# A three-stage mixer (decayed attention, two MLPs): attention products in whole float32, and the decays' range tests moved behind it

## The chip, the cores and the metric

One core of a Trainium2 chip runs the whole program in one launch. The time is device microseconds of that core, the median of 3 runs.

## The reference

Batch 4, 8 heads, 768 steps, head size 48 (384 = 8 x 48 channels).

```python
mag = np.sqrt(a_re**2 + a_im**2); scale = np.minimum(mag, 0.999) / (mag + 1e-6)
a = (a_re + 1j * a_im) * scale                       # decay per step and channel
for t in range(768):                                 # attention: a state per head
    S = a[t][:, None] * S + k[t][:, None] * v[t]     # complex S
    y[t] = q[t] @ S.real
x = y                                                # first MLP, with a low-rank mix over time
u = x + (x^T U V)^T;  x1 = u + relu(u @ w1) @ w2     # 384 -> 1536 -> 384
u = x1 + real(fft2(x1)); n = layernorm(u)            # second MLP
out = u + relu(n @ v1) @ v2
```

All inputs are float32, and the U, V and the weights of both MLPs arrive as 64-bit floats that the kernel turns into 32-bit ones itself.

## The kernel before, in words

Time is cut into chunks of 128 steps, 6 for a batch. `decays(m)` and `turns(m)` make, for a pair of chunks, the cumulated decay (a running product, L398) and the cumulated angle (a running sum, L440) and multiply both into q and k: the tile `QK`, which six transfers (L481) lay out as `QT` with the heads along the free axis. `products(m, j)` then does a chunk's matrix products: scores `sc` from `QT`, masked scores `pm`, the output `y` from `pm` and v and from the carried state `S`, and the state's growth `g` from the transposed key `k` and v.

Precision is kept in two ways. Batches 0 and 1 (`plain`) compute `y` in float32, each head in two halves of 64 columns. Batches 2 and 3 split both factors into a float16 part and its float16 rest (`ph`, `qh`, `vh`, `vl`, `Sh`, `Sl`) and add three float16 products. The growth `g` is made of three float16 products in all batches, from `scaled`, a copy of the key times the chunk's end decay (ACT, L477). ACT makes the float16 parts, and DVE the rests.

The MLPs (`moe_units`) run batch after batch in 24 units (2 halves of the sequence x 12 blocks of 128 hidden channels). A unit is 9 float16 products into `hp`, a relu split into `hh` (ACT, L232) and `hl` (DVE, L233), and 9 products into `acc` (L214, L215, L200). The attention of batch b+1 is interleaved with the first MLP of batch b. With the first MLP of batch 3 run the Fourier transform of batch 0 (`dft`) and the conversion of the second MLP's weights (`weights(1)`): 24 pieces `stw` are loaded as 64-bit words (L129), and ACT, DVE (L122, L144, L145) and GpSimd (L167, L168) turn each into `w`.

Order on each engine is set by a scheduler, which takes the instructions in the order of the code and by priority, and lets one with less priority go ahead where its inputs are there and the buffers free. What runs first is then fixed. A pool's tag names a ring of buffers: tag `u` (5 buffers) holds the MLP's input pieces `u` (three alive at a time), the loaded weight pieces `stw` and the keys `k` of batch 0.

Range tests leave sums and maxima in `stats`, and `verdict` reads them at the end: whether the decays lie in the range that the method allows (inside `decays`, L345 to L371) and whether the weights do (`check_w`, L178).

Of the kernel before, what the change touches and what calls it, by code (L numbers as in the profile page):

```python
# [22 lines left out]
DM = H * D  # L23
# [5 lines left out]
KSCALE = 2.0**10  # L29
VSCALE = 2.0**10  # L30
GSCALE = 2.0**-10
YSCALE = 2.0**-10 / FSCALE
# [18 lines left out]
def mixer_kernel(ctx, tc, a_in, qk_in, v_in, u_in, v4_in, w_in, cc_in, ss_in, cb_in, sb_in, id_in, mask_in, rows_in, out):  # L51
# [26 lines left out]
    def pair(name):  # L78
        return moe.tile([128, 2, 384], F16 if parts16[0] else F32R, tag="u", name=name, bufs=5)
# [92 lines left out]

    def check_w(mi, f, z):

        hi = wt[mi, f][:, 0, z * 384 : (z + 1) * 384]
        unread = ft(f"chk{mi}_{f}_{z}", [128, 384], BF16, tag="chk", bufs=2)
        at = stats[:, list(BOUNDS).index(("w1", "w2")[z]), mi * FB + f : mi * FB + f + 1]
        V.scalar_tensor_tensor(out=unread, in0=hi, scalar=1.0, in1=hi, op0=ALU.mult, op1=ALU.mult, accum_out=at)  # L178
# [11 lines left out]
    def moe_units(mi, uT, finish, extra, batches=range(B)):  # L190
# [53 lines left out]
        "im": [(ALU.is_le, 0.0)],  # L244
# [68 lines left out]
    def decays(m):  # L313
# [17 lines left out]
        ew[m] = T_, Th, qf, kf, ends, a if b == 0 else turn, qk if b == 0 else ls  # L331
# [4 lines left out]
        def unread(js):  # L336
            n = (js.stop - js.start) * 384
            return slot(f"un{m}").bitcast(BF16)[:, :n].rearrange("p (i j t) -> p i j t", i=3, t=128)

        at_once = b or m in (0,1,)  # L340

        def steady(js):

            re, s2_ = of(js, a[:, 0], s2)
            V.scalar_tensor_tensor(  # L345
                out=unread(js), in0=s2_, scalar=RE_LEAST, in1=re, op0=ALU.add, op1=ALU.is_le, accum_out=stat("re", b, cc[js.start])
            )

        def least_re(js):

            (re,) = of(js, a[:, 0])
            V.tensor_scalar(unread(js), re, RE_LEAST, 0.0, ALU.is_ge, ALU.add, accum_out=stat("re", b, cc[js.start]))

        def most_im(js):
            (s2_,) = of(js, s2)
            V.tensor_scalar(unread(js), s2_, IM_MOST**2, 0.0, ALU.subtract, ALU.max, accum_out=stat("im", b, cc[js.start]))

        for js in jj:
            re, im, s1_, s2_ = of(js, a[:, 0], a[:, 1], s1, s2)
            if at_once:  # L360
                if b == 0:
                    V.scalar_tensor_tensor(out=s2_, in0=im, scalar=0.25, in1=im, op0=ALU.mult, op1=ALU.mult)
                else:
                    A.activation(s2_, im, AF.Square, scale=0.5)
                A.activation(s1_, re, AF.Square, accum_out=stat("big", b, cc[js.start]))
                if m == 0:
                    steady(js)
                else:
                    unused = unread(js) if b == 0 else Th[:, :, js]
# [3 lines left out]
            else:  # L373
                (V if m == 0 else G).tensor_tensor(s2_, im, im, ALU.mult)
                A.activation(s1_, re, AF.Square, accum_out=stat("big", b, cc[js.start]))
                (G if m == 2 else V).tensor_tensor(s1_, s1_, s2_, ALU.add)
                most_im(js)
# [3 lines left out]
        for js in jj:  # L381
# [4 lines left out]
            if not at_once:  # L386
                least_re(js)
# [35 lines left out]
    def turns(m):  # L423
# [3 lines left out]
        T_, Th, qf, kf, ends, turn, scaled = ew[m]  # L427
# [6 lines left out]
        for js in jj:  # L434
# [31 lines left out]
            for j in range(js.start, js.stop):  # L466
                c = cc[j]
                where = dict(pl=early[0], bufs=1) if b == 0 and c % 3 == 2 else dict(bufs=2)
# [13 lines left out]
                qkt[b, c] = QT, scaled[:, :, :, j]  # L482
                yield

    def products(m, j):
# [5 lines left out]
        plain = b <= 1  # L491
        at = attention_pool()

        def t3(nm, bufs, shape, dt=F32):
            return at(f"{nm}{n}", nm, bufs, shape, dt, attp[1] if dt == F16 else attp[0])

        QT, scaled = qkt[b, c]
        vin = inp["v", b, c]
        sc, pm, kp = [], [], []
        pool = pacc if b == 0 else pms  # L500

# [7 lines left out]
        def masked(hf):  # L509
            pm.append(room[:, hf] if b == 0 else at(f"pm{n}_{hf}", "pm", 2, (128, 4, 128)))  # L510
            V.tensor_tensor(pm[hf], sc[hf], mask.unsqueeze(1).to_broadcast([128, 4, 128]), ALU.mult)
            if not plain:
                hs = slice(hf * 4, hf * 4 + 4)
                A.copy(ph[:, hs], pm[hf])
                V.tensor_tensor(plo[:, hs], pm[hf], ph[:, hs], ALU.subtract)

        def turned(z):
            kp.append(bank(f"kp{n}_{z}", pool)[:, :384])
            for i in range(3):
                T.transpose(kp[z][:, i * 128 : (i + 1) * 128], scaled[:, z, i], ident)  # L520

        def split(z):
            src = kp[z].rearrange("t (x h) -> t h x", h=8)
            dh, dl = (k.rearrange("t (h z x) -> t h z x", h=8, z=2)[:, :, z, :] for k in (kh, kl))
            A.activation(dh, src, AF.Copy, scale=KSCALE)
# [768 lines left out]
```

## Time and profile before

| | |
|---|---|
| median of 3 runs (lowest, highest) | 995.34 us (994.02, 997.83) |
| the profiled execution: own time, span | 995.69 us, 993.9 us |
| busy in the span: PE, DVE, ACT, POOL | 819.1, 669.9, 465.4, 259.9 us |

The span is the time from the first to the last instruction of the profiled execution. PE is the matrix engine (PEld its weight loads), DVE the vector engine, ACT the scalar engine, POOL is GpSimd, SP issues transfers. Busy times of engines overlap each other.

### The profile page before, as it was taken

The numbers are of one execution on the slowest core, as the hardware profiler recorded it, in microseconds if no ns is written. First come the engines' busy times: TensorE is split into PE (matmuls) and PEld (weight loads), VectorE is DVE, ScalarE is ACT, GpSimd is POOL, SyncE is SP. The second block draws the span as 40 slices with busy tenths as digits, with TensorE's granted clock in tenths as the row PEclk, the third lists the DMA queues.
The fourth block names the chain that finished last, engine by engine and source line by source line (L and its number), as shares of the span: only waits on it lengthen the run. The fifth ranks groups of instructions, "written<-read, shape, count | busy, mean of one in ns | idle before, by whom it ended". The sixth has DMA issues, their size and how long they took to land.

```text
span 993.9 us, 16380 instructions
## 1 busy us (share of the span) xinstructions
PE 819.1 (82%) x6350; PEld 550.5 (55%) x6350; DVE 669.9 (67%) x1214; ACT 465.4 (47%) x897; POOL 259.9 (26%) x275
## 2 busy tenths in 40 slices
PE   0056667777897886989979799879999999999997
PEld 0045534556565654656656466446666765666564
DVE  7966797867567787858876996995645454463221
ACT  8546457576775867767753253332222211312111
POOL 4412474412012010111102644761322132020000
PEclk9999878888998999999989999999999999999999
DMA  9059646453743727264262632420101021000000
GB/s 360 1 64 146 159 130 139 106 101 97 115 90 81 111 73 128 68 102 86 37 89 74 221 96 87 145 64 24 50 31 48 1 80 50 1 25 1 25 24 28
DMA packets 47095, 83.41 MB, mean 84 GB/s; under 512 B 5600, under 2 KB 36064, under 8 KB 47008
## 3 DMA queue, kind: packets, MB, share of 16 engines
q1 hardware_dynamic: 45152, 75.96, 34.0%
q0 software_dynamic: 1856, 6.31, 1.8%
q8 instruction: 52, 0.85, 0.4%
q14 instruction: 35, 0.29, 0.1%
HBM read 53.79 MB, written 9.44 MB: 64 GB/s over the span
## 4 chain that ended last, share of the span: by engine, by line
PE 37%; DVE 30%; DMA 13%; ACT 9%; issue 5%; SPq 3%; POOL 2%; DVEq 0%; ACTq 0%; POOLq 0%
DMA QT<-QK 8%; PE acc L214 5%; PE acc L200 5%; PE acc L215 5%; PE hp L105 5%; PE hp L107 5%; PE hp L106 5%; DMA stw<-in_w_dram 4%; SPq L481 3%; DVE ls L398 2%; DVE wxw L145 2%; DVE wxw L144 2%; PE sc L506 2%; DVE hl L233 2%; DVE chk L178 2%
## 5 line engine op out<-in xcount | busy, mean ns | idle before, releaser
L214 PE MATMUL acc<-w,hh 128*128 128x384 f16 x576 | 194.5, 338 | 26.4 <-ACT hh L232 25.1
L233 DVE SCALAR_TENSOR_TENSOR hl<-hp,hh 128x384 f16<-128x384 f32 x192 | 105.1, 550 | 156.1 <-ACT hh L232 155.3
L232 ACT ACTIVATE hh<-hp 128x384 f16<-128x384 f32 x192 | 92.7, 484 | 231.9 <-PE hp L107 214.2
L215 PE MATMUL acc<-w,hh 128*128 128x384 f16 x576 | 193.6, 337 | 0.0
L200 PE MATMUL acc<-w,hl 128*128 128x384 f16 x576 | 128.8, 332 | 1.0 <-DVE hl L233 1.0
L105 PE MATMUL hp<-u,w 128*128 128x384 f16 x288 | 95.1, 333 | 13.3 <-ACT u L691 8.3
L506 PE MATMUL sc<-QT 96*128 96x128 f32 x384 | 62.8, 324 | 45.2 <-DMA QT<-QK 25.2
L106 PE MATMUL hp<-u,w 128*128 128x384 f16 x288 | 95.4, 331 | 2.2 <-DVE u L692 2.2
L214 PEld LDWEIGHTS <-hh 128*128 128x128 f16 x576 | 57.9, 100 | 69.8 <-ACT hh L232 33.8
L105 PE MATMUL hp<-n,w 128*128 128x384 f16 x288 | 93.9, 326 | 1.5 <-DVE hl L233 1.5
L107 PE MATMUL hp<-u,w 128*128 128x384 f16 x288 | 94.7, 330 | 0.0
L106 PE MATMUL hp<-n,w 128*128 128x384 f16 x288 | 93.9, 326 | 0.0
L107 PE MATMUL hp<-n,w 128*128 128x384 f16 x288 | 93.9, 326 | 0.0
L506 PEld LDWEIGHTS sc<-QT 96*128 96x128 f32 x384 | 57.6, 230 | 50.3 <-issue 40.8
L106 PEld LDWEIGHTS <-w 128*128 128x128 f16 x576 | 56.7, 98 | 43.9 <-issue 10.2
L105 PEld LDWEIGHTS <-w 128*128 128x128 f16 x576 | 56.8, 99 | 43.3 <-issue 7.7
L200 PEld LDWEIGHTS <-hl 128*128 128x128 f16 x576 | 57.1, 100 | 41.6 <-issue 3.7
L107 PEld LDWEIGHTS <-w 128*128 128x128 f16 x576 | 56.7, 98 | 39.6 <-issue 4.3
L215 PEld LDWEIGHTS <-hh 128*128 128x128 f16 x576 | 58.0, 101 | 35.9 <-issue 6.4
L581 POOL TENSOR_SCALAR fe<-QT 96x8 f32<-96x8 f32 x20 | 5.2, 263 | 215.2 <-DMA QT<-QK 215.2
L168 POOL TENSOR_TENSOR w<-wxw,w 128x384 f16<-128x384 f32 x48 | 54.1, 1131 | 3.1
L520 PE MATMUL kp<-ident,qkin 128*128 128x128 f32 x30 | 6.1, 338 | 55.0 <-ACT qkin L477 53.9
(290 smaller groups left out, 1728.0 us busy)
## 6 DMA issues: line engine op xcount, KB each, us to landing
QT<-QK SPq DMA_DIRECT2D x144, 129.0 KB
stw<-in_w_dram SPq DMA_DIRECT2D x48, 384.0 KB
ain<-in_a_dram SPq DMA_DIRECT2D x12, 768.0 KB
qkin<-in_qk_dram SPq DMA_DIRECT2D x12, 768.0 KB
x1d<-x SPq DMA_DIRECT2D x24, 192.0 KB
vin<-in_v_dram SPq DMA_DIRECT2D x18, 192.0 KB
lo<-x1d SPq DMA_DIRECT2D x12, 192.0 KB
out_dram<-lo SPq DMA_DIRECT2D x12, 192.0 KB
```

The costliest lines, as they stand in the source:

```text
L105: T.matmul(o, ah, bh, start=start, stop=False, skip_group_check=skip)
L106: T.matmul(o, ah, bl, start=False, stop=False, skip_group_check=skip)
L107: T.matmul(o, al, bh, start=False, stop=stop, skip_group_check=skip)
L144: V.scalar_tensor_tensor(out=xi, in0=xi, scalar=3, in1=low, op0=ALU.logical_shift_left, op1=ALU.bitwise_or)
L168: G.tensor_tensor(w[:, 1, zs], x, w[:, 0, zs], ALU.subtract)
L200: T.matmul(acc[t], hl[:, t * 128 : (t + 1) * 128], w2h, start=False, stop=f == FB - 1 and extra is None)
L214: T.matmul(acc[t], hh[:, ts], w2h, start=f == 0, stop=False)
L215: T.matmul(acc[t], hh[:, ts], w2l, start=False, stop=False)
L232: A.activation(hh, hp, AF.Relu)
L233: V.scalar_tensor_tensor(out=hl, in0=hp, scalar=0.0, in1=whole_of(hh), op0=ALU.max, op1=ALU.subtract)
L481: nc.sync.dma_start(QT[p0 : p0 + 16], QK[:, z, i, :])
L506: T.matmul(ps[:, h, :], q[:, 128:256], q[:, :128], start=True, stop=True)
```

## The change

All products of the attention become float32: `y` in all batches as before in batches 0 and 1, and `g` from the whole key and v, in two halves (64 and 32 columns). The float16 parts and rests of scores, queries, values, keys and state go. The key is transposed as it is in `QK`; the end decay is applied to the state after the growth is added (it was applied to the old state before). The tests of the decays leave `decays`; `check_a` loads the decays once more and tests them, in code that stands in the second MLP's first batch. Buffers: `stw`, the keys `k` of all batches and the decays of `check_a` share a ring `st` of 3; `u` has its 5 to itself; the third `QK` and `QT` buffer, that batch 0 had, is there for all batches.

```diff
     def fetch(src, name):
-        st = moe.tile([128, 384, 2], I32, tag="u", name=f"st{name}", bufs=5)[:, :n]
+        st = moe.tile([128, 384, 2], I32, tag="st", name=f"st{name}", bufs=3)[:, :n]
...
+    def check_a(m, z):
+
+        b, cc = PAIRS[m]
+        x = moe.tile([128, 768], F32, tag="st", name=f"rl{m}_{z}", bufs=3)
+        nc.sync.dma_start(x, a_in[b, cc[0] // 2][:, z].rearrange("p i j t -> p (i j t)"))
+        unread = slot(f"chka{m}_{z}").bitcast(BF16)
+        if z == 0:
+            V.tensor_scalar(unread, x, RE_LEAST, 0.0, ALU.is_ge, ALU.add, accum_out=stat("re", b, cc[0]))
+            A.activation(unread, x, AF.Square, accum_out=stat("big", b, cc[0]))
+        else:
+            for c, sign in zip(cc, (1.0, -1.0)):
+                V.tensor_scalar(unread, x, sign, 0.0, ALU.mult, ALU.max, accum_out=stat("im", b, c))
...
-                    A.activation(unused, re, AF.Relu, bias=least, scale=-1.0, accum_out=stat("im", b, cc[0]))
-                    A.activation(unused, s2_, AF.Relu, bias=most, accum_out=stat("im", b, cc[1]))
-                V.scalar_tensor_tensor(out=s1_, in0=s2_, scalar=4.0, in1=s1_, op0=ALU.mult, op1=ALU.add)
...
+            A.activation(s2_, im, AF.Square)
+            A.activation(s1_, re, AF.Square)
+            (G if m == 2 else V).tensor_tensor(s1_, s1_, s2_, ALU.add)
...
-                if c != NC - 1:
-                    for i in range(3):
-                        A.activation(scaled[:, :, i, j], QK[:, :, i, 128:256], AF.Copy, scale=ends[:, i, j : j + 1])
...
-            A.activation(dh, src, AF.Copy, scale=KSCALE)
-            V.scalar_tensor_tensor(out=dl, in0=src, scalar=KSCALE, in1=dh, op0=ALU.mult, op1=ALU.subtract)
+            A.copy(ks.rearrange("t (h z x) -> t h z x", h=8, z=2)[:, :, z, :], src)
...
-            ops = [(lambda h: ph[:, h], vh), (lambda h: ph[:, h], vl), (lambda h: plo[:, h], vh)]
-                ops += [(lambda h: qh[:, h], shi), (lambda h: qh[:, h], slo), (lambda h: ql[:, h], shi)]
-        summed(yp, ops, halves=plain)
+        summed(yp, ops)
...
-            summed(gp, [(hs(0), vh), (hs(0), vl), (hs(768), vh)])
+            summed(gp, [(lambda h: ks[:, h * 96 : (h + 1) * 96], vin)])
...
-                V.scalar_tensor_tensor(out=sS, in0=gp[:96], scalar=scale, in1=sS, op0=ALU.mult, op1=ALU.add)
+                V.scalar_tensor_tensor(out=sS, in0=gp, scalar=FSCALE, in1=S, op0=ALU.mult, op1=ALU.add)
+                V.tensor_tensor(by_head(sS), by_head(sS), f3, ALU.mult)
...
+        if b == 0 and half == 1:
+            check_a(f, g)
```

Three places in the order of the instructions. First DVE in the attention of batch 2, chunks 1 and 2, while the first MLP works on batch 1 (`hl`). Before:

```order
L526 SCALAR_TENSOR_TENSOR k_1_2979<-kp_1_1_3004,k_1_2979 128x8x48
L372 SCALAR_TENSOR_TENSOR ls_4_3159<-ls_4_3159 128x768
L556 SCALAR_TENSOR_TENSOR vl_2_3214<-vin_2_3012,vh_2_3213 128x384
L619 SCALAR_TENSOR_TENSOR S_1_3097<-g_1_3096,S_1_3097 96x384
L608 TENSOR_TENSOR S_2_3372<-S_1_3097,fe_2_3278 96x384
L233 SCALAR_TENSOR_TENSOR hl_1_0_5_2920<-hp_1_0_5_2902,hh_1_0_5_2919 128x384
L565 TENSOR_TENSOR ql_2_3232<-QT_2_2988,qh_2_3231 96x1024
L511 TENSOR_TENSOR pm_2_0_3227<-sc_2_0_3208,mask 128x512
L624 TENSOR_TENSOR Sl_1_3131<-S_1_3097,Sh_1_3130 96x384
```

After:

```order
L546 SCALAR_TENSOR_TENSOR S_1_2851<-g_1_2828,S_0_2684 96x384
L547 TENSOR_TENSOR S_1_2851<-S_1_2851,fe_1_2761 96x384
L446 TENSOR_TENSOR QK_4_3080<-ls_4_2879,turn_4_2878 128x6x128 x2
L244 SCALAR_TENSOR_TENSOR hl_1_0_2_2523<-hp_1_0_2_2512,hh_1_0_2_2522 128x384
L359 SCALAR_TENSOR_TENSOR ls_0_3259<-ls_0_3259 128x768
L480 TENSOR_TENSOR pm_2_0_2940<-sc_2_0_2926,mask 128x512
L244 SCALAR_TENSOR_TENSOR hl_1_0_3_2562<-hp_1_0_3_2535,hh_1_0_3_2561 128x384
```

The rests are gone from DVE's queue, and the masked score of chunk 2 stands three units earlier in the MLP.

Second the transfer queue (SP) where the second MLP's weights begin to be loaded. Before:

```order
L481 DMA QT_5_4969<-QK_5_4967 16x8x258 x6
L851 DMA rows<-in_rows_dram 128x5
L861 DMA lo_0_5704<-x1d_75 128x384
L861 DMA lo_1_5705<-x1d_75 128x384
...
L129 DMA stw_0_0_5663<-in_w_dram 128x768
L129 DMA stw_0_1_5720<-in_w_dram 128x768
```

After:

```order
L450 DMA QT_5_4383<-QK_5_4381 16x8x258 x5
L309 DMA vin_5_4603<-in_v_dram 128x384
L127 DMA stw_0_0_4967<-in_w_dram 128x768
L127 DMA stw_0_1_5024<-in_w_dram 128x768
L127 DMA stw_1_0_5079<-in_w_dram 128x768
```

The weights now follow the last `QT` directly, ahead of the Fourier transform's loads.

Third DVE early in the first MLP's last batch (units 3 to 7 of batch 3). Before:

```order
L145 SCALAR_TENSOR_TENSOR wxw_2_0_5867<-stw_2_0_5865,wxw_2_0_5867 128x384
L233 SCALAR_TENSOR_TENSOR hl_3_0_4_5862<-hp_3_0_4_5833,hh_3_0_4_5861 128x384
L122 TENSOR_SCALAR stw_2_1_5902<-stw_2_1_5902 128x384
L178 SCALAR_TENSOR_TENSOR chk_2_0_8671,stats<-w_831 128x384
L144 SCALAR_TENSOR_TENSOR wxw_2_1_5904<-wxw_2_1_5904,stw_2_1_5902 128x384
L145 SCALAR_TENSOR_TENSOR wxw_2_1_5904<-stw_2_1_5902,wxw_2_1_5904 128x384
L122 TENSOR_SCALAR stw_3_0_5943<-stw_3_0_5943 128x384
L233 SCALAR_TENSOR_TENSOR hl_3_0_5_5899<-hp_3_0_5_5884,hh_3_0_5_5898 128x384
```

After:

```order
L143 SCALAR_TENSOR_TENSOR wxw_11_1_6052<-stw_11_1_6050,wxw_11_1_6052 128x384
L178 TENSOR_SCALAR chka_0_6159,stats<-rl_0_6157 128x768
L244 SCALAR_TENSOR_TENSOR hl_3_0_4_5166<-hp_3_0_4_5137,hh_3_0_4_5165 128x384
L178 TENSOR_SCALAR chka_0_6193,stats<-rl_0_6191 128x768
L244 SCALAR_TENSOR_TENSOR hl_3_0_5_5203<-hp_3_0_5_5188,hh_3_0_5_5202 128x384
L178 TENSOR_SCALAR chka_0_6239,stats<-rl_0_6237 128x768
L178 TENSOR_SCALAR chka_0_6271,stats<-rl_0_6269 128x768
L178 TENSOR_SCALAR chka_0_6307,stats<-rl_0_6305 128x768
L244 SCALAR_TENSOR_TENSOR hl_3_0_6_5244<-hp_3_0_6_5225,hh_3_0_6_5243 128x384
```

The last weight conversion (`wxw_11_1`) is done by unit 3 of that batch, and the tests of the decays (`chka`, of the loaded `rl`) stand there, not in the second MLP where their code is written.

## Rows read from the trace of the kernel before

**Rows 1.** Stretches: length, busy us (instructions) by engine, granted PE clock, DMA share, GB/s.

```profile
0.00:62.00 62.00, 1.54 (x6) 0.94 (x6) 50.70 (x64) 39.95 (x69) 23.81 (x25) 1.00 0.48 157
62.00:567.00 505.00, 411.76 (x3750) 289.76 (x3750) 381.37 (x610) 315.88 (x595) 124.29 (x111) 0.92 0.53 106
567.00:667.00 100.00, 87.36 (x543) 54.78 (x543) 88.41 (x192) 40.90 (x88) 61.41 (x70) 0.97 0.36 107
667.00:994.00 327.00, 318.44 (x2054) 205.04 (x2052) 149.40 (x350) 68.65 (x147) 50.42 (x69) 0.99 0.09 30
```

**Rows 2.** Timeline of ACT: first relu of batch 3, and of the second MLP.

```profile
567.09 0.85 ACT L232 ACTIVATE hh<-hp 128x384 f16<-128x384 f32 x2
...
666.69 0.47 ACT L232 ACTIVATE hh<-hp 128x384 f16<-128x384 f32 x1
```

**Rows 3.** The chain that ended last, by engine (page).

```profile
PE 37%; DVE 30%; DMA 13%; ACT 9%; issue 5%; SPq 3%; POOL 2%; DVEq 0%; ACTq 0%; POOLq 0%
```

**Rows 4.** Groups by line: name xcount | busy us, mean ns | idle before.

```profile
L526 DVE SCALAR_TENSOR_TENSOR k<-kp,k 128x384 f16<-128x384 f32 x40 | 21.4, 546 | 1.7 <-ACT k L525 1.5
L515 DVE TENSOR_TENSOR ph<-pm,ph 128x512 f16<-128x512 f32 x24 | 16.2, 681 | 1.7 <-ACT ph L514 1.7
L565 DVE TENSOR_TENSOR ql<-QT,qh 96x1024 f16<-96x1024 f32 x10 | 14.6, 1456 | 9.9 <-ACT qh L564 9.6
L556 DVE SCALAR_TENSOR_TENSOR vl<-vin,vh 128x384 f16<-128x384 f32 x17 | 13.4, 789 | 1.5 <-PE g L534 1.5
L477 ACT ACTIVATE ls<-QK,fe 128x256 f32<-128x256 f32 x45 | 19.6, 498 | 2.6 <-DVE QK L474 2.6
L514 ACT CAST ph<-pm 128x512 f16<-128x512 f32 x24 | 14.5, 613 | 11.3 <-DVE pm L511 11.2
L564 ACT CAST qh<-QT 96x1024 f16<-96x1024 f32 x10 | 10.4, 1041 | 28.4 <-DMA QT<-QK 21.7 <-issue 3.7 <-PE y L534 2.9
L371 ACT ACTIVATE turn<-ls,most 128x768 f32<-128x768 f32 x9 | 8.4, 932 | 0.1
```

**Rows 5.** Pieces of the chain in order of time: start us, us, what.

```profile
7.88 0.92 ACT un L370 x2
...
492.91 0.47 DVE Sl L624
```

**Rows 6.** Timeline of PE: float32 and float16 products of the attention.

```profile
226.50 1.14 PE L534 MATMUL y<-vin,pm 128*64 128x48 f32 x32 [0.48 <-DVE k L526]
227.47 0.75 PE L534 MATMUL y<-S,QT 96*64 96x48 f32 x20
228.16 0.20 PE L534 MATMUL g<-vh,k 128*128 128x48 f16 x1
228.28 0.32 PE L534 MATMUL y<-S,QT 96*64 96x48 f32 x2
228.53 0.20 PE L534 MATMUL g<-vh,k 128*128 128x48 f16 x1
...
350.72 0.36 PE L534 MATMUL y<-vh,ph 128*128 128x48 f16 x8
350.93 0.36 PE L534 MATMUL y<-vl,ph 128*128 128x48 f16 x8
```

**Rows 7.** The chain by line, from 148 to 205 us.

```profile
by line: DMA stw<-in_w_dram 36.8%; issue 8.5%; DVE stw L122 6.8%; DVE QK L474 5.9%; DVE wxw L144 5.6%; DVE wxw L145 4.8%; DVE vl L556 3.5%; DVE pm L511 3.3%; DVE unv L646 3.1%; DVE turn L440 2.9%; DVE hl L233 2.7%; DVE k L526 2.5%; ACT wxw 
```

**Rows 8.** Groups by line: a weight piece's conversion on DVE, and the weights' test.

```profile
L145 DVE SCALAR_TENSOR_TENSOR wxw<-stw,wxw 128x384 int32<-128x384 int32 x48 | 34.3, 717 | 0.4
L144 DVE SCALAR_TENSOR_TENSOR wxw<-wxw,stw 128x384 int32<-128x384 int32 x48 | 34.2, 713 | 1.0 <-ACT wxw L122 0.7
L122 DVE TENSOR_SCALAR stw<-stw 128x384 int32<-128x384 int32 x48 | 24.1, 502 | 19.5 <-DMA stw<-in_w_dram 19.4
L178 DVE SCALAR_TENSOR_TENSOR chk<-w 128x384 bf16<-128x384 f16 x48 | 31.1, 684 | 0.9 <-PE y L534 0.8
```

**Rows 9.** By tile: a test of 128x768 decays on DVE (min/median/max ns).

```profile
L352 DVE TENSOR_SCALAR_CACHE_REDUCE un<-ain x1: 943/943/943, 11.9 to 11.9; 128x768 bf16<-128x768 f32 x1
```

More of the change, by code (lines that the diff above doesn't have):

```diff
@@ L330, in decays @@
         jj = [slice(0, 2)]
-        ew[m] = T_, Th, qf, kf, ends, a if b == 0 else turn, qk if b == 0 else ls
+        ew[m] = T_, Th, qf, kf, ends, a if b == 0 else turn
         def of(js, *xs):
             return [x[:, :, js] for x in xs]
[L336 to L347, printed above, removed]
@@ L426, in turns @@
         at = attention_pool()
-        T_, Th, qf, kf, ends, turn, scaled = ew[m]
+        T_, Th, qf, kf, ends, turn = ew[m]
         use(TRIG)
@@ L467, in turns @@
                 c = cc[j]
-                where = dict(pl=early[0], bufs=1) if b == 0 and c % 3 == 2 else dict(bufs=2)
+                where = dict(pl=early[0], bufs=1) if c % 3 == 2 else dict(bufs=2)
                 QK = at(f"QK{b}_{c}", "QK", shape=(128, 2, 3, 258), **where)
@@ L490, in products, with t3 @@
         last = c == NC - 1
-        plain = b <= 1
         at = attention_pool()
-        def t3(nm, bufs, shape, dt=F32):
-            return at(f"{nm}{n}", nm, bufs, shape, dt, attp[1] if dt == F16 else attp[0])
-        QT, scaled = qkt[b, c]
+        def t3(nm, bufs, shape):
+            return at(f"{nm}{n}", nm, bufs, shape)
+        QT, QK = qkt[b, c]
         vin = inp["v", b, c]
@@ L500, in products @@
         pool = pacc if b == 0 else pms
+        halves = slice(0, 64), slice(64, 128)
         def scores(hf):
@@ L519, in turned, with summed @@
             for i in range(3):
[L520 to L522 removed]
+                T.transpose(kp[z][:, i * 128 : (i + 1) * 128], QK[:, z, i, 128:256], ident)
             src = kp[z].rearrange("t (x h) -> t h x", h=8)
[L524 to L528 removed]
+            A.copy(ks.rearrange("t (h z x) -> t h z x", h=8, z=2)[:, :, z, :], src)
+        def summed(out, ops):
             for o, (l, r) in enumerate(ops):
@@ L532, in summed @@
                     hsl = slice(h * 48, (h + 1) * 48)
-                    for p in (slice(0, 64), slice(64, 128)) if halves else (slice(0, l(h).shape[-1]),):
+                    for p in halves:
+                        p = slice(p.start, min(p.stop, l(h).shape[-1]))
                         T.matmul(
@@ L548, in products @@
         scored.append(nc.cur_bb.bb.instructions[-1])
-        if b == 0 and not last:
-            vs = slot(f"v{n}").bitcast(F16).rearrange("p (z m) -> p z m", z=2)
-            vh, vl = vs[:, 0], vs[:, 1]
-        elif b:
-            vh, vl = t3("vh", 2, (128, DM), F16), t3("vl", 1, (128, DM), F16)
-        if not (plain and last):
-            A.activation(vh, vin, AF.Copy, scale=VSCALE)
-            V.scalar_tensor_tensor(out=vl, in0=vin, scalar=VSCALE, in1=vh, op0=ALU.mult, op1=ALU.subtract)
-        if not plain:
-            ph, plo = t3("ph", 1, (128, 2, 8, 128), F16).rearrange("p s h t -> s p h t")
         yield
@@ L561, in products @@
         masked(0)
-        if not plain and c > 0:
-            qh, ql = t3("qh", 1, (96, 8, 128), F16), t3("ql", 1, (96, 8, 128), F16)
-            A.copy(qh, QT[:, :, :128])
-            V.tensor_tensor(ql, QT[:, :, :128], qh, ALU.subtract)
         yield
@@ L616, in products @@
             if S is None:
-                A.activation(sS, gp[:96], AF.Copy, scale=scale)
+                V.scalar_tensor_tensor(out=by_head(sS), in0=by_head(gp), scalar=FSCALE, in1=f3, op0=ALU.mult, op1=ALU.mult)
             else:
-                V.scalar_tensor_tensor(out=sS, in0=gp[:96], scalar=scale, in1=sS, op0=ALU.mult, op1=ALU.add)
-            state[b] = sS
-            if not plain:
-                shi, slo = t3("Sh", 1, (96, DM), F16), t3("Sl", 1, (96, DM), F16)
-                A.copy(shi, sS)
-                V.tensor_tensor(slo, sS, shi, ALU.subtract)
-                state[b] = sS, shi, slo
+                V.scalar_tensor_tensor(out=sS, in0=gp, scalar=FSCALE, in1=S, op0=ALU.mult, op1=ALU.add)
@@ L1016, in mixer_kernel @@
     going = going.rearrange("p i t -> p (i t)")
-    first = ExitStack()
-    early[0] = first.enter_context(tc.tile_pool(name="early", bufs=3))
+    early[0] = apool.enter_context(tc.tile_pool(name="early", bufs=3))
     for kind in ("a", "qk"):
@@ L1034, in mixer_kernel @@
                 T.matmul(warm, mask, wide.bitcast(F16), start=True, stop=True, skip_group_check=True)
-    first.close()
-    early[0] = None
-    attp[1] = apool.enter_context(tc.tile_pool(name="halves", bufs=1))
     for b, g, f, half in moe_units(0, lambda b, g: uts[b, g], finish1, extra1):
```

95 lines of the change are left out of this document (21 added, 74 removed).

## The prediction

> **What bounds the kernel now.** I first cut the span at two events: the first relu of the first MLP's batch 3 at 567 us and the first relu of the second MLP at 667 us [rows 2]. The busy times in the stretches [rows 1] (the engines stand in the order PE, PEld, DVE, ACT, POOL) then tell three stories.
>
> Behind 667 us PE is busy 318 of 327 us at nearly the full clock, and DVE not half. PE is the bound there, and only products of the MLP and of the Fourier transform stand there, which the change leaves alone. Between 62 and 567 us, where attention and first MLP share the engines, nobody is full: PE 412 of 505 us, DVE 381, ACT 316, and PE's granted clock is 0.92 on average of its two levels. That stretch is a net of waits. From 567 to 667 us DVE is the fullest with 88 of 100 us: it converts the second MLP's weights, folds for the Fourier transform and makes the relu's rests, and PE, with 87 us busy, waits for it now and then.
>
> The chain of work that ended last agrees: PE has 37% of it, nearly all of that in the last third, DVE 30%, transfers 13%, ACT 9% [rows 3]. So what DVE and ACT lose before 567 us is worth something wherever it lies on the chain, and what DVE gains between 567 and 667 us costs something.
>
> **What is removed.** On DVE the rests of the keys (40 instructions, 21.4 us), of the masked scores (24, 16.2 us), of the queries (10, 14.6 us) and of the values (17 of one name, 13.4 us); together 65.6 us. On ACT the scaled keys (45 of one name, 19.6 us), the float16 scores (14.5 us), queries (10.4 us) and the relus that test the decays (8.4 us in the row, and a second set of the same shape, 9 more); together 61 us or more [rows 4]. Some smaller groups (the state's parts, the values' float16 parts) go as well. All of it lies before 567 us.
>
> How much of that ends the kernel earlier? I followed the chain from 0 to 567 us and took every piece whose line is removed: 58 pieces, the first at 7.88 us, the last at 492.91 us [rows 5], 39.7 us in all. **This is the first term, -39.7 us.** It is between two bounds. If another chain lies just below this one everywhere, much less comes back, say half, 20 us. If on the other side the stretch stays as full for DVE as it is, more comes back; that bound is worked out below under the rivals.
>
> **What is added on PE.** In the built program the attention has 1008 float16 products of 48 columns fewer (480 of `g`, 528 of `y`) and 672 float32 half products more (320 and 352). A float16 one costs 25.6 ns start to start: eight from 350.72 to 350.93 us, 0.205 us. A float32 one is two records in the trace, and 32 records start between 226.50 and 227.47 us, so 30.3 ns for a record and 60.6 ns for a product [rows 6]. Removed 1008 x 25.6 = 25.8 us, added 672 x 60.6 = 40.7 us: PE gets +14.9 us.
>
> One saving stands against it. Where a float32 `y` product and a float16 `g` product alternate, the pair takes 0.37 us (228.16 to 228.53 us) [rows 6] instead of 0.086, so each change of type costs about 0.14 us. The order before has 47 such changes between `g` and `y`, and the changed kernel has none; 47 x 0.14 = 6.7 us come back. PE's net is +8.2 us. Cover for it are PE's waits in that stretch, 93 of 505 us [rows 1]; I charge PE's share of the chain, 37% [rows 3], and **this term is +3 us** (bounds 0 and +15).
>
> A rule of the Trainium skill speaks against this part as well (FP8 and Floating Point Precision, section TensorE Precision Notes): a true float32 product is four passes through the array, against the three of a float16 pair with its rests. By it the removed 25.8 us would become 34.4 and PE's gross would be +8.6 us instead of +14.9, and the third term of 3 us near 1. The rows say more than the rule, since a half product of 64 columns fills less of the array; I stay with the rows.
>
> **What is moved.** In the order of before one weight piece of the second MLP has been converted on DVE when batch 3 of the first MLP begins, and in the changed one 18 of 24, since `stw` no longer shares its ring with `u` and the attention is through sooner. A piece is 0.72 + 0.71 + 0.50 = 1.93 us of DVE [rows 8], so 17 pieces, 33 us, leave the stretch from 567 to 667 us. Into it come the 36 tests of the decays, 0.94 us each [rows 9], 34 us. The weights' tests (0.65 us each [rows 8]) change places too: 24 stood before 567 us and 11 behind it, and now 38 stand in that stretch, 27 more, 17.5 us. Together 34 + 17.5 - 33 = +18 us on an engine that has 11.6 us free there [rows 1]. **The term is +6 us** (0 if the conversion's waits for transfers go with it; the other bound is a rival). The 12 squares of the tests on ACT cost nothing: ACT has 59 us free in that stretch. The 33 us that now come earlier fall where DVE loses 66 us and where it had 124 us free [rows 1].
>
> **The ring of the weights.** From 148 to 205 us, 36.8% of the chain, 21 us, is waiting for a weight piece from memory [rows 7]. Of the five buffers of `u` three are held by the MLP's inputs, so two pieces can be under way; now it is three. From none to two thirds of the 21 us could go; I take a third, **-7 us**. The keys of batch 1 borrow from the same three buffers, so I don't take more.
>
> **Sum.** -39.7 + 3 + 6 - 7 = -37.7 us. The profiled execution took 995.69 us, of which the span is 993.9; it would become 958. It lies 0.35 us above the median of the runs shown, so I forecast **957.6 us**.
>
> Nothing on the state's path speaks against it. The end decay is now multiplied behind the addition, one more DVE instruction per chunk in series, but the scaled copy of the key (three ACT instructions of 0.5 us) falls out ahead of the transposes [rows 4], so that the path from `QK` to the state gets shorter.
>
> **The rivals.**
>
> *More than the chain shows.* DVE loses 66 us and the tests of the weights (24 x 0.65, 16 us) before 567 us, and gets 33 us of conversions: net -49 us. It has 432 us of work in 567 us [rows 1], 76%; at the same fullness the stretch shrinks by 64 us, and with the +6 the time is 937 us. For it: nobody is full there, so the waits follow the work. Against it: PE's 420 us would then have to fit into 441 us, 95%, through all the waits of the attention. Chance 0.17.
>
> *Another chain takes over.* Transfers and their issue hold 16% of the chain [rows 3], the `QT` transfers above all, and they stay. If they lie just below, half of the 39.7 us comes back and nothing of the ring's 7: -20 + 3 + 6, 984 us. Chance 0.17.
>
> *The tests of the decays hold up the MLP.* They stand in DVE's queue ahead of the relus' rests, and each waits for a load of 384 KB into a ring of three. From 148 to 205 us ten pieces were converted, and the chain waited 21 us for such loads [rows 7], 2.1 us a load. If each of the 24 loads did that in the last batch, it would be 50 us, and the time 995.3 - 37.7 + 50 = 1008 us. It decides from 1.6 us a load on. Against it: the transfers have two thirds of their time free there (share 0.36) [rows 1], no weights stand behind in that ring, and a load needs nothing from any engine but its buffer. Chance 0.07.
>
> *The gain and the new work cancel*, within 5 us: both of the last two by halves. Chance 0.04.
>
> **How the numbers follow.** The likeliest case has the remaining 0.55 and its own range from 940 to 973 us (first term between 55 and 25 us). I put the range to 926 and 986 us: it takes in the second and most of the first of the other cases, and leaves out the slow case. 0.5% (5 us) is about what a measurement can tell. Faster by more than that: 0.55 + 0.17 + 0.16 = 0.88; within: 0.05; slower: 0.07.
>
> **What would show it.** In the changed profile: the first relu of batch 3 some 40 us earlier, near 525 us; PE's busy time up by no more than 10 us in spite of its new products; `g` and `y` at 30 ns a record without 0.37 us pairs; the stretch from there to the second MLP about as long as now, with DVE nearly full and the tests of the decays in it; the last 327 us unchanged. I am wrong if that stretch gets longer by tens of us with DVE waiting for `rl`, or if the first relu of batch 3 moves by less than 20 us while the waits for `QT` grow.

## The result and the profile after

The changed kernel took 1001.29 us, the median of 20 runs (996.76 to 1004.34), beside 994.62 us for the kernel before (990.12 to 999.16, 20 runs): ratio 1.0061, 95% interval 1.0046 to 1.0075. It is slower by 0.6%. Its profiled execution, from which the rows below come, took 996.76 us, the shortest of its 20 runs. The forecast of 957.6 us was 44 us too low, and the time is outside its range.

The two events that cut the span stood at 567.09 and 666.69 us [rows 2]. In the changed kernel, on the timeline of ACT (start, duration, instruction):

```profile
567.53 0.48 ACT L243 ACTIVATE hh<-hp 128x384 f16<-128x384 f32 x1
...
668.77 0.49 ACT L243 ACTIVATE hh<-hp 128x384 f16<-128x384 f32 x1 [9.43 <-PE hp L105]
```

They have hardly moved (0.4 and 2.1 us later), although batch 0 of the first MLP begins 10 us earlier (138.2 against 148.1 us). So what was gained by 138 us was lost again before 567 us, together with what the removed work should have given there. The stretches of the changed kernel, in the columns of [rows 1]:

```profile
0.00:62.00 62.00, 4.83 (x21) 4.46 (x22) 47.48 (x59) 35.87 (x54) 21.73 (x23) 1.00 0.52 165
62.00:567.50 505.50, 461.90 (x4091) 326.98 (x4090) 342.14 (x521) 262.65 (x466) 141.88 (x142) 0.94 0.53 118
567.50:668.80 101.30, 87.37 (x530) 53.72 (x530) 92.44 (x245) 33.13 (x77) 29.05 (x36) 0.97 0.46 139
668.80:995.00 326.20, 317.46 (x2047) 204.29 (x2045) 152.33 (x360) 69.77 (x147) 50.64 (x69) 0.99 0.08 28
```

DVE and ACT did lose their work: 342 us for 381, 263 for 316. But PE is busy 461.9 us of 505.5 where it was 411.8, at a slightly higher clock. By the forecast it was to get 8 us more, and it got 50. What fills it is seen on the page, in the chain by engine (PE had 37% in [rows 3]) and in the row of `g` (line, name, count, busy us and mean ns, idle time before):

```profile
PE 57%; DVE 21%; DMA 11%; issue 4%; ACT 4%; SPq 2%; POOL 0%; DVEq 0%; ACTq 0%
...
L496 PE MATMUL g<-vin,k 128*32 128x48 f32 (+1 forms) x640 | 81.0, 238 | 0.3 <-ACT k L487 0.3
```

The timeline of PE, in a stretch like that of [rows 6], shows why (the time from one row's start to the next's is what its records cost):

```profile
337.84 1.14 PE L496 MATMUL y<-vin,pm 128*64 128x48 f32 x32
338.81 0.79 PE L496 MATMUL y<-S,QT 96*64 96x48 f32 x20
339.39 0.48 PE L496 MATMUL g<-vin,k 128*64 128x48 f32 x4
339.81 0.33 PE L496 MATMUL y<-S,QT 96*64 96x48 f32 x4
339.96 0.48 PE L496 MATMUL g<-vin,k 128*64 128x48 f32 x4
...
341.09 2.27 PE L496 MATMUL g<-vin,k 128*64 128x48 f32 x20
343.29 0.34 PE L225 MATMUL acc<-w,hh 128*128 128x384 f16 x1
```

32 records of `y` take 0.97 us, 30 ns each, as forecast. 20 of `g` take 2.20 us, 110 ns each. A head of `g` has 96 key columns, which `halves` cuts into 64 and 32, two records each: the width of the weights' tile changes inside every head and from head to head. From start to start, the four records of a head take 93, 152, 67 and 136 ns in the median (64 to 64 columns, 64 to 32, 32 to 32, 32 to 64): 0.45 us, where four records of `y` take 0.12. Over the whole trace the 640 records of `g` take 73.2 us from start to start (gaps over 1 us counted as 1 us), 43.8 us more than in the first experiment below, where only the cut differs. Among the records of `y` and `g` there are 307 changes of width.

The last batch's stretch grew little, from 99.6 to 101.2 us, but its chain of waits is not that of before. Before, from 567 to 667 us, and in the changed kernel, from 567.5 to 668.8:

```profile
by line: DMA stw<-in_w_dram 13.2%; DVE wxw L145 11.1%; DVE wxw L144 9.9%; issue 7.3%; DVE hl L233 7.2%; DVE stw L122 6.1%; DVE chk L178 4.7%; DVE ee L891 4.7%; DVE un L971 3.9%; DVE f L872 3.3%; POOL lo L943 2.5%; POOL w L168 2.4%; DVE eel 
...
by line: DVE chk L189 20.0%; DMA rl<-in_a_dram 17.5%; DVE chka L182 15.7%; DVE hl L244 8.0%; issue 6.5%; DVE chka L178 3.8%; DVE x L637 3.7%; DVE wxw L142 3.5%; DMA stw<-in_w_dram 3.1%; DVE stw L120 2.9%; DVE st L871 2.8%; DVE wxw L143 1.7%
```

Tests of the decays (`chka`), the waits for their loads (`rl`) and tests of the weights (`chk`) hold more than half of it now.

### The profile page after: what moved, and what is told of

The parts are those of the page before. It is cut to its first block, busy times and chain, and to the rows that moved or that the text cites. A ratio compares the mean times of both kernels' runs of the same rounds, so it can differ in the third digit from the quotient of the medians.

```text
span 995.0 us, 16878 instructions
## 1 busy us (share of the span) xinstructions
PE 871.6 (88%) x6686; PEld 589.4 (59%) x6686; DVE 634.4 (64%) x1180; ACT 401.4 (40%) x742; POOL 243.3 (24%) x268
## 4 chain that ended last, share of the span: by engine, by line
PE 57%; DVE 21%; DMA 11%; issue 4%; ACT 4%; SPq 2%; POOL 0%; DVEq 0%; ACTq 0%
PE acc L225 6%; PE acc L226 6%; PE acc L211 6%; PE hp L103 6%; PE hp L105 6%; PE hp L104 6%; PE g L496 6%; PE y L496 4%; PE sc L475 4%; DMA stw<-in_w_dram 4%; DMA ain<-in_a_dram 3%; DVE chk L189 2%; DMA QT<-QK 2%; DVE wxw L142 2%; DMA rl<-in_a_dram 2%
## 5 line engine op out<-in xcount | busy, mean ns | idle before, releaser
L225 PE MATMUL acc<-w,hh 128*128 128x384 f16 x576 | 189.7, 331 | 12.0 <-ACT hh L243 11.4
L226 PE MATMUL acc<-w,hh 128*128 128x384 f16 x576 | 189.5, 331 | 1.8 <-POOL w L166 1.8
L104 PE MATMUL hp<-n,w 128*128 128x384 f16 x288 | 95.0, 330 | 5.0 <-DVE n L902 5.0
L103 PE MATMUL hp<-n,w 128*128 128x384 f16 x288 | 94.5, 329 | 1.8 <-DVE hl L244 1.4
L105 PE MATMUL hp<-n,w 128*128 128x384 f16 x288 | 95.1, 330 | 0.0
L225 PEld LDWEIGHTS <-hh 128*128 128x128 f16 x576 | 56.8, 99 | 51.9 <-ACT hh L243 16.6
L496 PE MATMUL g<-vin,k 128*32 128x48 f32 (+1 forms) x640 | 81.0, 238 | 0.3 <-ACT k L487 0.3
L226 PEld LDWEIGHTS <-hh 128*128 128x128 f16 x576 | 57.1, 99 | 36.1 <-issue 4.8
L475 PEld LDWEIGHTS sc<-QT 96*128 96x128 f32 x384 | 55.5, 216 | 27.3 <-issue 22.1
L496 PEld LDWEIGHTS g<-vin,k 128*32 128x32 f32 (+1 forms) x640 | 56.4, 129 | 18.1 <-ACT k L487 1.1
L485 PE MATMUL kp<-ident,QK 128*128 128x128 f32 x120 | 20.9, 287 | 49.6 <-DVE QK L446 49.1
```

What stands on the lines that cost most here:

```text
L103: T.matmul(o, ah, bh, start=start, stop=False, skip_group_check=skip)
L104: T.matmul(o, ah, bl, start=False, stop=False, skip_group_check=skip)
L105: T.matmul(o, al, bh, start=False, stop=stop, skip_group_check=skip)
L225: T.matmul(acc[t], hh[:, ts], w2h, start=f == 0, stop=False)
L226: T.matmul(acc[t], hh[:, ts], w2l, start=False, stop=False)
L475: T.matmul(ps[:, h, :], q[:, 128:256], q[:, :128], start=True, stop=True)
```

## The experiments

One table first: where each kernel's profiled execution spends its time, cut at the first relu of the first MLP's batch 0 (the front lies ahead of it), of its batch 3 (the last batch begins) and of the second MLP (the rest). "e1, padded" is kernel e1 with that edit, and so on. The stretches are us of one execution; medians and ratios (to the kernel before, run on the same chip) are the measurement. Differences of medians below join runs of several chips, whose medians of the kernel before lie between 994.4 and 996.4 us, and most intervals reach 2 to 5 us to either side; a difference of that size is not settled.

| kernel | median us | ratio (95%) | front | batches 0 to 2 | last batch | rest |
|---|---|---|---|---|---|---|
| before | 994.62 | | 148.1 | 419.0 | 99.6 | 327.2 |
| changed | 1001.29 | 1.0061 (1.0046 to 1.0075) | 138.2 | 429.4 | 101.2 | 326.2 |
| e1 `g` 64+64 | 975.94 | 0.9816 (0.9787 to 0.9846) | 133.4 | 409.0 | 101.6 | 328.7 |
| e2 `g` 96 | 999.96 | 1.0057 (1.0032 to 1.0081) | 133.4 | 439.7 | 101.5 | 329.7 |
| e3 `g` 32+32+32 | 1023.85 | 1.0305 (1.0255 to 1.0354) | 130.8 | 460.6 | 102.2 | 327.2 |
| e4 before, `g` 64+64 | 994.65 | 1.0006 (0.9988 to 1.0024) | 146.7 | 415.8 | 101.5 | 327.1 |
| e13 e1, padded (POOL) | 983.98 | 0.9874 (0.9843 to 0.9906) | 142.0 | 420.4 | 94.3 | 326.3 |
| e16 e1, padded (ACT) | 971.62 | 0.9760 (0.9730 to 0.9789) | 138.1 | 401.7 | 102.6 | 328.9 |
| e5 e1, no tests | 959.52 | 0.9639 (0.9604 to 0.9674) | 133.1 | 407.4 | 89.9 | 325.1 |
| e8 e1, tests in attention | 969.08 | 0.9735 (0.9692 to 0.9777) | 126.8 | 423.0 | 89.8 | 325.3 |
| e15 changed, tests in attention | 989.70 | 0.9952 (0.9928 to 0.9976) | 132.9 | 438.8 | 87.9 | 327.6 |
| e6 e1, tests late | 963.20 | 0.9694 (0.9659 to 0.9729) | 133.7 | 407.4 | 86.2 | 332.1 |
| e11 e1, decays ahead | 968.40 | 0.9717 (0.9690 to 0.9744) | 134.6 | 401.0 | 101.0 | 329.1 |
| e12 control of e11 | 975.92 | 0.9822 (0.9785 to 0.9859) | 133.2 | 411.3 | 101.6 | 326.8 |
| e14 e11 and e6 | 947.62 | 0.9545 (0.9497 to 0.9592) | 133.5 | 397.6 | 84.8 | 331.2 |
| e17 e14 and e16 | 951.71 | 0.9559 (0.9528 to 0.9589) | 135.6 | 401.0 | 84.1 | 331.6 |

**The width of `g`.** The theory: PE pays for each change of the tile's width. The rivals: narrow products are slow in themselves, or PE is not what bounds and the moved tests are. First, `g` in 64 and 64 columns, reading 32 columns of the next head into rows that nobody uses (the last head stays 64 and 32):

```diff
-            gp = bank(f"g{n}")[:96, :DM]
-            summed(gp, [(lambda h: ks[:, h * 96 : (h + 1) * 96], vin)])
+            gw = bank(f"g{n}")[:, :DM]
+            gp = gw[:96]
+            summed(gw, [(lambda h: ks[:, h * 96 : min(h * 96 + 128, 768)], vin)])
```

> The growth g of the changed kernel, cut into 64 and 64 columns instead of 64 and 32 (the columns beyond 96 are the next head's and are not read; the last head keeps 64 and 32). Theory 1, a change of the tile's width in PE costs: in the trace of the changed kernel a head's four records of g take 0.448 us instead of 0.121, with a gap at each change between 64 and 32 columns. Then g's records come at about 31 ns, g takes some 26 us of PE instead of 75, PE's busy time falls from 872 to about 825 us, and the time from 1001 to 955 to 965 us. Theory 2, float32 products of g are slow for themselves (their weights, their place), and PE was not what held the kernel: g stays near 110 ns a record and the time within 5 us of 1001.

25.3 us came back for a cut that has the same number of products and more columns. The timeline of PE, where `y` and `g` alternate (26 changes of width are left in the whole trace):

```profile
198.20 0.32 PE L496 MATMUL g<-vin,k 128*64 128x48 f32 x4
198.31 0.32 PE L496 MATMUL y<-S,QT 96*64 96x48 f32 x4
198.43 0.32 PE L496 MATMUL g<-vin,k 128*64 128x48 f32 x4
198.55 0.32 PE L496 MATMUL y<-S,QT 96*64 96x48 f32 x4
```

Four records in 0.117 us, 29 ns each, for `g` and `y` alike. The time still missed the expectation by some 11 us; the runs on the tests show more of what holds it. Then `g` whole, in one piece of 96 columns (`(slice(0, 96),)` for `halves`):

> The growth g with a head's 96 columns in one float32 product, no halves. Theory 1: no change of width inside g, but one wherever g follows y (64 columns) or is followed by it; 320 records of perhaps 60 to 110 ns, 20 to 35 us, and some tens of changes at 0.14 us, so 965 to 985 us. Theory 2 (slow for itself): half the records of the changed kernel at the same 110 ns, g at 40 us, and the time still near 1000 us because PE does not hold it.

No faster than the changed kernel, and 15 us above theory 1's range. On the timeline of PE:

```profile
198.61 0.37 PE L496 MATMUL g<-vin,k 128*96 128x48 f32 x2
198.91 0.32 PE L496 MATMUL y<-S,QT 96*64 96x48 f32 x2
199.15 0.37 PE L496 MATMUL g<-vin,k 128*96 128x48 f32 x2
```

From start to start a `g` record in a row took 85 ns in the median, the step from `y` to `g` 152 and the one back 178 ns: half as many records, each dearer. In three pieces of 32 columns:

> The growth g in three products of 32 columns a head, so one width within g, that of the slow product of the changed kernel. Theory 1: 960 records at some 30 ns, 29 us, and changes of width only where y and g meet: 965 to 985 us. Theory 2, with 32 columns slow in themselves: 960 records at 105 ns, 100 us, and 1015 to 1030 us.

The time is what the rival expected and 39 us above theory 1's range, but the records refute the rival. The timeline of PE in two places:

```profile
193.91 0.88 PE L496 MATMUL g<-vin,k 128*32 128x48 f32 x48
...
248.51 0.32 PE L496 MATMUL y<-vin,pm 128*64 128x48 f32 x2
248.76 0.27 PE L496 MATMUL g<-vin,k 128*32 128x48 f32 x2
248.96 0.32 PE L496 MATMUL y<-vin,pm 128*64 128x48 f32 x2
```

48 narrow records in a row end after 0.88 us, under 20 ns each: they are the cheapest of all. Two of `y` and two of `g` in turn take 0.45 us: every `g` has another width than `y` now, and wherever the scheduler interleaves the two the width changes.

The records do not explain the time of these two kernels, though. From start to start over the whole trace, `y` and `g` together take 105.8 us in e2 and 122.6 in e3, less than the 130.5 of the changed kernel (84.1 in e1), with 110 and 215 changes of width for its 307. What does differ is the granted clock from 62 us to batch 3: 0.90 and 0.88 on average, where the changed kernel has 0.94 and e1 0.93 (columns as in [rows 1], e2 and then e3):

```profile
62.00:573.10 511.10, 454.75 (x3774) 324.49 (x3773) 341.84 (x522) 261.74 (x468) 139.60 (x142) 0.90 0.54 116
62.00:591.40 529.40, 473.70 (x4398) 329.58 (x4398) 344.05 (x524) 263.77 (x468) 141.62 (x143) 0.88 0.51 113
```

Whether the clock is the whole cause, and what lowers it, stays open. So e2 and e3 show what a record costs; what the changes of width cost the kernel is shown by e1, by e15 against e8 and, less surely, by e16 below. Last, the kernel before with its float16 `g` of batches 0 and 1 cut at 64 columns (`halves=plain`), so that `y` and `g` differ in type but not in width:

> The kernel before, with g's float16 products of batches 0 and 1 in two halves of 64 columns, as its float32 y. There a y and a g in alternation take 0.37 us, which the prediction put down to the change of type. If it is the width (theory 1), the gap goes though the types still alternate: a y (two records) and a g (now two) in 0.12 us. If it is the type, such a pair still takes 0.3 us or more. The time moves little either way, 985 to 1000 us: some 6 us of changes less, 240 products of 25 ns more.

On the timeline of PE the pairs that took 0.37 us in [rows 6] now take less than 0.1 us:

```profile
230.02 0.19 PE L534 MATMUL g<-vh,k 128*64 128x48 f16 x2
230.05 0.24 PE L534 MATMUL y<-S,QT 96*64 96x48 f32 x1
230.05 0.22 PE L534 MATMUL g<-vh,k 128*64 128x48 f16 x2
230.12 0.22 PE L534 MATMUL y<-S,QT 96*64 96x48 f32 x1
```

From a `y` record to a `g` record it is 31.5 ns in the median. So the 0.14 us that the prediction put down to the type is the width's. The whole time is unchanged, which says little: the edit adds 240 products, and `y` and `g` together still take 69.7 us for 71.5.

One change of width was left in e1, at the last head. The padded kernel gives that head 32 zero columns, written by POOL:

> The g-in-64-columns kernel with the last head's weights widened by 32 zero columns, so that no product of y or g is 32 columns wide: 20 times the change from 64 to 32 columns and back goes (each about 0.14 us, less the 0.03 us of a product in a row). If changes of width cost what the records said, TensorE is busy 4 to 5 us less, and the whole falls by 1.5 to 4 us, to 972 to 974.5. If the cost of g was that of narrow products in a row and not of changes, it stays at 975 to 977.

It got slower than e1, by 8 us. POOL's waits up to 145 us have a row that e1 does not have (us, times, longest):

```profile
POOL k L518 <- PE g L496: 8.6, 2, 7.8
```

POOL stands in its queue for the tile, and the attention's work on POOL behind it; the front is 8.6 us longer than in e1. Whether that wait is the whole cause is not shown: batches 0 to 2 are 11 us longer too, and the last batch 7 us shorter. That run says nothing on width. With the zeros written by ACT, which writes the rest of that tile anyway:

> The last head's weights widened by 32 zero columns, as in the padded kernel before, but written by ScalarE, which writes the rest of the same tile next to it, so that GpSimd gets no wait (it had waited 8.6 us for the tile behind g, and the front had become 8.6 us longer). Theory 1 (changes of width cost): TensorE busy 4 us less than with 32 columns in the last head, 971 to 975. Theory 2 (no effect of width at this place, or the time of the front is set by the order): 975 to 984.

4.3 us faster than e1, as theory 1 had it, though the two intervals touch. PE's busy time can't confirm it: 830.7 us for 836.2 in e1, but e12 below, with e1's products, has 831.0. The records of `g` do confirm it: they take 25.0 us from start to start, for 29.4 in e1 and 29.3 in e12. The front is longer by 5 us all the same, and that stays unexplained.

**The place of the tests.** e1 without any test of the decays (the call of `check_a` left out):

> The g-in-64-columns kernel without any range test of the decays (they are left out, with their second loads). If the moved tests cost what the stretch of the second MLP's first batch shows (101.6 us there against 99.6 in the kernel before), that stretch falls to 97 to 99.5 us and the whole to 972 to 974. If the tests and the waits of their loads were on the path for most of what the chain of waits gives them (the test lines and the loads of rl stand in that stretch's chain for more than a third of 101 us), the stretch falls below 90 us and the whole to about 960, which would make the move the second cause of the lost gain.

The second case came true: the tests cost 16.4 us (975.9 - 959.5); of the profiled executions' difference, 11.8 us lie in the last batch's stretch and 3.6 in the second MLP's first batch. The two stretches in the windows, of e1 and then of the kernel without the tests (columns as above):

```profile
542.30:644.00 101.70, 87.97 (x530) 54.29 (x530) 92.02 (x242) 33.34 (x76) 28.88 (x35) 0.95 0.46 138
644.00:727.20 83.20, 79.92 (x523) 52.23 (x521) 48.68 (x126) 18.64 (x40) 18.47 (x24) 1.00 0.08 25
```

```profile
540.40:630.30 89.90, 83.23 (x530) 53.53 (x530) 78.25 (x214) 24.48 (x54) 32.27 (x40) 1.00 0.15 45
630.30:709.90 79.60, 79.60 (x523) 52.44 (x521) 35.36 (x82) 17.15 (x38) 13.83 (x19) 1.00 0.10 33
```

Without them PE is busy 83 of 90 us there, for 88 of 102. No run tells the waits for the loads of `rl` from the work of the tests on DVE. The tests back in the attention, as before the change (old lines of `decays`, one load):

> The g-in-64-columns kernel with the range tests of the decays back in the attention, as they stood before the change; products stay float32, decays loaded once. Theory 1 (the move of the tests is the part that pays in the front): the front goes from 133 back to 144 to 148 us, the second MLP's first batch gives back 2 us, the attention's stretches lose a few us to ScalarE's two tests of 0.93 us for each pair of chunks: 983 to 992 us. Theory 2 (the tests were hidden beside other work in the attention, the chain pieces counted for them were not worth their length): 974 to 979.

969.1, 7 us less than with the tests moved, and below either expectation. The tests in the attention cost 9.6 us (969.1 - 959.5), and moved 16.4. The front is even shorter with them, 126.8 us; why the order there is better stays open. The same with the narrow `g` of the changed kernel:

> The changed kernel with g still in 64 and 32 columns, and the range tests of the decays back in the attention. Theory 1 (the two failed steps add): the move cost 7 us where g was in 64 columns, so without it 992 to 996. Theory 2 (where TensorE is the bound through the attention, the tests stand beside it, and the last batch gives its 12 us back): 986 to 991. Theory 3 (the move paid with the narrow g, since VectorE's and ScalarE's work in the attention fell): above 1000.

989.7 us, in the range of theory 2. The move costs 11.6 us here and 6.9 with the wide `g`. That the attention, where PE has more to do, gives less back for the work taken out of it would fit the stretches (batches 0 to 2 are 9.4 us shorter by the move here, and 14.0 with the wide `g`), but the two differ by less than their intervals. The other way round, the narrow `g` costs 20.6 us with the tests in the attention (e15 against e8) and 25.3 with the tests moved. Then e1 with the tests held behind the last DVE instruction of their own step of the second MLP, where DVE's load is lower:

```diff
-            check_a(f, g)
+            v = [i for i in nc.cur_bb.bb.instructions if i.engine == V.engine][-1]
+            with tc.issue_after(v):
+                check_a(f, g)
```

> The g-in-64-columns kernel with each load and test of the decays held back until VectorE's last instruction of its own step of the second MLP, so that none of it stands in the first MLP's last batch. Leaving the tests out had given 959.5, so they cost 16 us. Theory 1 (their place costs: they and their loads stand among the conversions of the last first-MLP batch, where the chain runs through VectorE): that batch goes from 101.7 back to about 90 us, VectorE has room in the second MLP, 960 to 966. Theory 2 (VectorE's work itself costs, wherever it stands, since the transforms of the next batch and the products' splits wait behind it): the second MLP's first batch is longer by what the other one gains, 971 to 978.

12.7 us came back. The same two stretches of this kernel:

```profile
541.10:627.30 86.20, 80.38 (x517) 52.08 (x517) 55.64 (x116) 24.43 (x55) 30.57 (x40) 1.00 0.20 60
627.30:710.80 83.50, 82.42 (x537) 53.74 (x536) 62.05 (x152) 27.79 (x63) 13.74 (x19) 1.00 0.42 131
```

DVE has 62 of 83.5 us in the second MLP's first batch and holds PE up little: PE is busy 82.4 of them. Held back there, the tests of the decays cost 3.7 us (963.2 - 959.5) and not 16.4, so it is mostly their place that costs. The edit moves more than it says, though: the weights' tests (`chk`) leave the last batch as well. Their work on DVE in that stretch (two records a test), in e1, in e5 and in this kernel:

```profile
542.30:644.00 101.70, 21.19 (x72) 0.95 0.46 138
540.40:630.30 89.90, 24.70 (x96) 1.00 0.15 45
541.10:627.30 86.20, 0.00 (x0) 1.00 0.20 60
```

e5 has all of them in the last batch, and it takes 89.9 us all the same, so they cost little there without the decays' tests beside them. How the 12.7 us divide between the two kinds of tests is not shown.

**The load of the decays.** ACT's squares begin each pair's decays. Among ACT's waits (us, times, longest) they wait for the load, in the kernel before and in the changed one:

```profile
ACT ls L365 <- DMA ain<-in_a_dram: 4.0, 2, 3.1
...
ACT ls L349 <- DMA ain<-in_a_dram: 19.7, 9, 5.2
```

In e11 the decays get a second buffer and are loaded one pair earlier; the third buffer of `QK` and `QT` is kept for batch 0 only, to make room:

```diff
-            load("a", m + 1)
+            load("a", m + 2)
...
-                where = dict(pl=early[0], bufs=1) if c % 3 == 2 else dict(bufs=2)
+                where = dict(pl=early[0], bufs=1) if b == 0 and c % 3 == 2 else dict(bufs=2)
```

> The g-in-64-columns kernel with two buffers for the decays of the attention, so that each pair's load is issued one pair earlier; to make room, the third buffer of QK and QT is kept only for the first batch. Theory 1: ScalarE's squares waited 22.9 us for the loads of the decays, 9 times, and the chain of waits had about 21 us of it; with the load ahead this goes, 955 to 966 us. Theory 2: the chain passes to the next engine (VectorE's elementwise work, the TensorE products), or the third buffer of QK was worth as much: 972 to 982.

The wait falls to 3.8 us, 2 times, from 22.9 in e1, and the time by 7.5 us, less than either the wait or theory 1's range (955 to 966) had it. The control, with the third buffer gone and nothing else:

> The g-in-64-columns kernel with the third buffer of QK and QT for the first batch alone, as before the change; the decays have one buffer. It is the control of the kernel with the decays loaded ahead (968.4). Theory 1 (the load ahead brought the gain): 974 to 980, the third buffer is worth nothing or a little. Theory 2 (the scheduler's order with two buffers of QK brought it): 967 to 971.

975.9, as e1: the gain is the load's.

**Together.**

> The g-in-64-columns kernel with the decays loaded one pair ahead and their tests held back to the second MLP. If the two gains stand in different stretches, as the traces of the single edits say (-7.5 us by the load ahead, up to -16 by the tests' place), they add: 952 to 960. If the late tests hold up the second MLP: 964 to 970.

947.6 us, the fastest of all: 4.5% less than before. The sum of the single gains from e1 was 20 us, and 28 came; why more came stays open, and with intervals of up to 5 us part of it may be noise. Its stretches:

```profile
62.00:531.00 469.00, 413.75 (x4091) 294.07 (x4091) 345.29 (x522) 260.14 (x466) 143.46 (x142) 0.96 0.59 127
531.00:615.80 84.80, 80.29 (x518) 52.04 (x517) 55.79 (x116) 24.50 (x54) 30.63 (x40) 1.00 0.21 61
```

> All that the runs found, together: g in 64 columns with the last head widened by zero columns that ScalarE writes, the decays loaded one pair ahead, their tests held back to the second MLP. The widening gave 4.4 us by itself: 941 to 946 if it adds to the 947.6 of the other edits. If its ScalarE writes or the changed order cost in the front as in the first widened kernel: 948 to 956.

The padded head adds nothing that shows here: 951.7 us, with a ratio whose interval overlaps that of e14.

## Why the prediction was wrong

**The step that failed: what `g` costs on PE.** The prediction took "672 x 60.6 = 40.7 us", the price of a `y` product in 64 columns, for the 320 products of `g` too, that is 19.4 us. They took 73.2. With the wide `g` of e1, `y` and `g` together take 84.1 us from start to start, 12.6 more than the 71.5 of before and near the +8.2 that the prediction had for PE; with the narrow `g` it is 130.5, 59 more. No row of before has a 64-column product beside a 32-column one, so that price should have been bounded from both sides, and the upper bound stood in [rows 6]: the prediction read its 0.37 us pairs as a change of type and credited 6.7 us for their end. They are changes of width, and the change made hundreds more, 307 by the trace. From a 64-column record to the next 32-column one it is 0.15 us, and 0.14 back. The Trainium skill has the rule (TensorEngine Tiling (Array Packing), section Tiling Modes, Key Properties): changing the tiling mode drains the engine. The records agree that such a change costs; the price is theirs.

Its second half, PE's cover, failed with it. The term charged PE's work at 37%, its share of the chain of before over the whole span, although the prediction itself says that nearly all of that lies in the last third. From 62 to 567 us, where the new products stand, PE had 70.8 us of that chain, 14%; in the changed kernel it has 278.9 there, 55%, and in e1 36%. Of the 43.8 us that the cut alone costs, 25.3 arrived, 58%. A share of the chain does not stay when the term is large enough to move the bound, and that 58 lies near 55 may be luck.

**-39.7 for what is removed: too much.** With the wide `g` and the tests left out, the kernel took 959.5 us, 36.9 less than the runs of before beside it, which looks like the forecast's -37.7; that is luck, since it is made up of other parts. The profiled stretches give 15.0 us of it in the front, 11.6 in batches 0 to 2, and 9.7 in the last batch, where no piece of [rows 5] lies. So ahead of the last batch some 27 us came, where the prediction had -39.7 + 3 - 7 = -43.7. How the missing 17 us divide between the removed work and the ring is not shown; the wait for the decays' loads, below, would account for 7.5 us of them.

**+6 for the last batch: near as a net.** In e5 the moved conversions and the ring gave 9.7 us there, and in e1 the tests took 11.8 of it back, and 3.6 behind it; in the changed kernel the last batch is 1.6 us longer than before. The error is in what it was weighed against: taking the tests out of the attention gave 9.6 us, not their length, so the move by itself lost 6.9 us with the wide `g` and 11.6 with the narrow one. The mechanism of the third rival, loads of `rl` ahead of the MLP's rests, did come: they have 17.5% of that chain, 17.7 us or 0.74 us for each of 24 loads, below the 1.6 us from which it was to decide alone.

**-7 for the ring: gone where it was read, not over the span.** Waits for `stw` have 4.9% of the chain between 138 and 200 us, where they had 36.8% between 148 and 205 [rows 7]. Over the span they have 37.5 us of the chain for 39.0 before, so they moved elsewhere, and no run shows that the ring gave anything.

**Not in the prediction at all:** the wait for the decays' loads, worth 7.5 us by e11.

**The signs and the rivals.** What the prediction said of the span behind 567 us came true: the last batch about as long, with DVE at 92 of 101 us, and the rest unchanged. The first relu of batch 3 did not come earlier, but what its sign of being wrong expected with that, growing waits for `QT`, did not come: they fell from 8% of the chain to 2%. The rival in which gain and new work cancel comes nearest in size (+6.7 us, beyond its 5), but by another mechanism; in none of the four do PE's new products take the gain.

The account from before, on the runs beside each kernel: without either loss (e8) the change gives -27.3 us, and 969.1 us lies inside the forecast's range. The narrow `g` then costs 20.6 to 25.3 us and the move of the tests 6.9 to 11.6, by which is taken first. The two orders use the same four runs, so that their sums agree shows nothing more. Either loss alone would have left the kernel faster: e1 by 1.8%, e15 by 0.5%.

## What to carry to other kernels

Price a matmul with its neighbours: look for a row where the same widths follow one another as they will in the changed order, and if there is none, make the widths equal, by computing columns that nobody reads if need be. When work leaves a chain, ask which engine the chain passes to before charging new work at its old share. Work moved off a busy stretch must be pinned where the room is, since this scheduler starts what it sees ready earlier than the code has it.

## What the hardware showed that was not expected

- A change of the weights' tile width took 0.13 to 0.15 us from record to record (64 to 32 columns 152 ns, back 136; 64 float32 to 128 float16 columns 155, back 127), and 152 ns from 64 to 96 with 178 back, against 0.03 us for 64-column records in a row. A change of type at one width (e4) costs nothing that shows. The step to the second record at the new width was dearer too, 93 ns (64 columns) and 67 (32) in the changed kernel's `g`.
- In the stretches shown, records of 32 columns in a row took under 20 ns and records of 64 columns 29 to 30; those of 96 columns took 85 ns in the median. As means over the traces of e3, e1 and e2 it was 25, 37 and 110 ns. One piece of 96 columns was dearer than two of 64.
